# Splitting w2 in the second and third group, and w1 half an expert ahead

## The chip, the cores and the metric

The kernel runs on one core of a Trainium2 chip. The metric is the device time in microseconds of one execution, as the median of several runs. One execution was also recorded by the hardware profiler.

## The reference

Four batches of eight heads run a gated linear recurrence over 768 positions. Its result, reshaped to 3072 rows of 384, goes through four experts, each a two-layer network with a ReLU, weighted by normalised probabilities:

```python
for t in range(S):                                    # S = 768, D = 48
    state = alpha[:, :, t, :, None] * state + einsum('bhd,bhe->bhde', k[:, :, t], v[:, :, t])
    y[:, :, t] = einsum('bhd,bhde->bhe', q[:, :, t], state)
x = y.transpose(0, 2, 1, 3).reshape(3072, 384)
p = domain_probs / (domain_probs.sum(-1, keepdims=True) + 1e-09)
for e in range(4):                                    # w1: (4, 384, 1024), w2: (4, 1024, 384)
    h = maximum(x @ w1[e], 0)
    out += p[:, e:e + 1] * (h @ w2[e])
```

## The kernel before

**Units and groups.** The recurrence is cut into 24 units of 128 positions of one batch (`units`). Units are put into seven groups: two units in the first (`gi == 0`), four in each of the next five, two in the last (`gi == LAST == 6`). A task is one group through one expert; it is written (gi, e) here, so (1, 3) is the second group's fourth expert. The last two groups alternate expert by expert. A task is an *up* pass over eight column tiles of w1 (`up`, `fc` from 0 to 7) and a *down* pass over w2 (`down`).

**Precision by splitting.** From the second group on, each float32 product is made of three products of a faster type. A weight piece is split into three parts: `top` (rounded, made by ScalarE at L231), `rest` (VectorE, L233) and `both` (VectorE, L234). In the same way each hidden tile gets `top` by ScalarE's Relu (L739), `low` by VectorE (L761) and `dif` by VectorE (L766). The first group multiplies the whole weights in plain float32 (L731 up, L809 down), so it needs no parts.

**Pieces.** w1 and w2 are cut into 16 pieces each, four to an expert; a whole piece has 384 KB, its three parts 1152 KB. `load_piece(l, i)` puts a load on the SP queue: either of the whole (L214 for w1, L218 for w2), or of the three parts from `kept` in device memory (L195). `split_piece(l, i)` is a generator: its first step is ScalarE's L231, its second the two VectorE instructions and a store of the parts to `kept` on POOL's queue (L236). `background()` moves every open generator one step on and starts one more from the list `making`; it is called once behind each column tile of an up pass and at a few places of a down pass. So a split put on the list at tile `fc` has its ScalarE step behind that tile and its VectorE step behind the next.

**What is split when.** w1's 16 pieces are split during the first group, those of an expert while the expert is used: for the first and the fourth expert at tiles 1, 3, 5, 7, for the two others at tiles 2 and 5 and two in the down pass. Four w2 pieces, `EARLY` (the third and fourth of the second and third expert), are split in the first group too. The twelve others are split in the second group, each before the down pass that reads it; all 32 are stored, and from the third group on every piece is loaded as parts. The whole w2 pieces of the second, third and fourth expert of the second group lie in a buffer of the tag `hT`, of which there are four: the fourth hidden tile (column tiles 6 and 7) of the same expert takes that buffer next.

**Buffers.** Split w1 parts take turns in four buffers (tag `w1`), which the second group's loads of w1 parts use as well. At the end of the first group's last up pass the loads for (1, 0) go out in turn: w2 whole, w1 parts, w2 whole and so on. PSUM has four banks for products (`one`, `ops`; tag `g`) and two buffers for transposes, outputs and states (`tp`, `yps`, `sps`; tag `w`).

**Order.** The order of instructions on each engine is the order in which the program writes them. The attention of a unit is a generator of some 17 steps; `deal()` gives every step a due time on a clock of estimated matmul time, and `advance()` runs the steps that are due between matmuls. Loads of the raw q, k, v and alpha (`rq`, `rk`, `rv`, `ra`, L173) are written there and stand on SP's queue between those of the weights. A step's ScalarE copies are L503 (`qb`), L521 (`KT`), L598 and L602 (`lat`); VectorE's are L510, L512, L522 and L539; L667 to L670 update the state `st`.

Of the kernel before, what the change touches and what calls it, by code (L numbers as in the profile page):

```python
# [10 lines left out]
F32 = mybir.dt.float32  # L11
# [9 lines left out]
def kernel(  # L21
# [37 lines left out]
    nc = tc.nc  # L59

    B, H, S, D = q.shape
    E, DM, F = moe_w1.shape
# [9 lines left out]
    NQ = 4  # L72
# [69 lines left out]
    making = deque()  # L142
    splitting = []
# [17 lines left out]

    EARLY = {(1, 2), (1, 3), (2, 2), (2, 3)}


    def load(u, names):
# [3 lines left out]
        for nm in names:  # L171
# [4 lines left out]
    kept = [[dram.tile([P, 3, KC * QF], F32, name=f"kept{l}_{i}") for i in range(E * NQ)]  # L176
            for l in range(2)]
    wt = ({}, {})
    first_piece = lambda gi, e: (min(gi, LAST - 1) * E + e) * NQ

    AHEAD = 4


    SPLIT_AT = [(2, 5), (1, 3, 5, 7)]
    BESIDE = [{1: 2, 2: 3}, {2: 0, 4: 1}, {2: 0, 4: 1}, {2: 0, 3: 1, 4: 2, 5: 3}]

    def load_piece(l, i, beside=False):
        if i >= E * NQ * LAST:
            return
        gi, k = divmod(i, E * NQ)  # L190
        e, c = divmod(k, NQ)
        if gi > l or gi == 1 and (e, c) in EARLY:
            w = wt[l][i] = wts.tile([P, 3, KC * QF], F32R, name=f"w{l + 1}",
                                    bufs=AHEAD if l == 0 else NQ)
            nc.sync.dma_start(out=w.bitcast(F32), in_=kept[l][k])  # L195
            return
        if l == 1 and gi == 0 and not beside:
            return
        if l == 0:

            if e == 0:
                shared[c] = wts.tile([P, 3, KC * QF], F32R, name="w2", bufs=NQ)
            w = shared[c][:, 2 - e % 2].bitcast(F32)
        else:

            if gi == 1 and e > 0:
                if c == 0:
                    shared["w2"] = hid.tile([P, NQ, KC * QF], F32, name="hT", bufs=NQ)
                w = shared["w2"][:, c]
            else:  # L210
                w = hidden[c][:, gi].rearrange("p f n -> p (f n)")[:, :KC * QF].bitcast(F32)
        wt[l][i] = w
        if l == 0:
            nc.sync.dma_start(  # L214
                out=w.rearrange("p (c f) -> p c f", f=QF),
                in_=moe_w1[e].rearrange("(c p) f -> p c f", p=P)[:, :, c * QF:(c + 1) * QF])
        else:
            nc.sync.dma_start(  # L218
                out=w.rearrange("p (c d) -> p c d", d=DM),
                in_=moe_w2[e].rearrange("(c p) d -> p c d", p=P)[:, c * FPQ:(c + 1) * FPQ])  # L220

    def split_piece(l, i):
        k = i % (E * NQ)
        whole = wt[l].pop(i) if l == 0 else wt[l][i]
        if i >= E * NQ:
            w = wt[l][i] = wts.tile([P, 3, KC * QF], F32R, name="w2", bufs=NQ)
        else:
            w = wts.tile([P, 3, KC * QF], F32R, name="w1", bufs=AHEAD)
        top, both, rest = (w[:, part] for part in range(3))

        nc.scalar.activation(out=top, in_=whole, func=ACT.Copy, scale=LIFT)  # L231
        yield
        nc.vector.tensor_sub(rest, whole, top.bitcast(F32))  # L233
        nc.vector.scalar_tensor_tensor(out=both, in0=rest.bitcast(F32), scalar=4096.0, in1=whole,  # L234
                                       op0=ALU.mult, op1=ALU.add)
        nc.gpsimd.dma_start(out=kept[l][k], in_=w.bitcast(F32))  # L236

    def background():


        for piece in list(splitting):
            if next(piece, splitting) is splitting:
                splitting.remove(piece)
        if making and len(splitting) < 4:
            splitting.append(making.popleft())
            next(splitting[-1])
# [454 lines left out]
    def up(gi, e, fc, slots=None):  # L701
        n = len(groups[gi]) * P
        lo, hi = (slots.start * P, slots.stop * P) if slots else (0, n)
        begins, ends = lo == 0, hi == n
        c, f = divmod(fc, FPQ)
        i = first_piece(gi, e) + c
        if fc == 0 and begins:
            for k in range(NQ):
                hidden[k] = hid.tile([P, 3, FPQ, NT], F32R, name="hT", bufs=NQ)
        if gi == fc == 0 and begins:  # L710
            for k in range(NQ):
                load_piece(1, e * NQ + k, beside=True)
        if gi == 1 and fc in BESIDE[e]:
            making.append(split_piece(1, first_piece(gi, e) + BESIDE[e][fc]))
        if gi == 0 and ends and fc in SPLIT_AT[e in (0, E - 1)]:
            k = SPLIT_AT[e in (0, E - 1)].index(fc)
            making.append(split_piece(0, e * NQ + k))
        if gi == 0 and ends and e + 1 < E and fc == (0 if e == 0 else FCH // 2):
            for k in range(NQ):
                load_piece(0, (e + 1) * NQ + k)  # L720
        col = slice(f * P, (f + 1) * P)
        if gi > 0:
            w = wt[0][i].rearrange("p t (c f) -> p t c f", f=QF)[:, :, :, col]
        else:
            w = wt[0][i].rearrange("p (c f) -> p c f", f=QF)[:, :, col]
        parts = [hidden[c][:, part, f, lo:hi] for part in range(3)]
        whole = parts[2].bitcast(F32)
        one = ps.tile([P, NT], F32, name="one", tag="g", bufs=4)[:, :hi - lo]
        if gi == 0:
            for kc in range(KC):  # L730
                nc.tensor.matmul(one, lhsT=w[:, kc], rhs=xraws[gi][:, kc, lo:hi],  # L731
                                 start=(kc == 0), stop=(kc == KC - 1))
            nc.scalar.activation(out=whole, in_=one, func=ACT.Relu)
        else:
            for part in (1, 2, 0):
                for kc in range(KC):
                    nc.tensor.matmul(one, lhsT=w[:, part, kc], rhs=x_part(gi, part, kc),  # L737
                                     start=(part == 1 and kc == 0), stop=(part == 0 and kc == KC - 1))
            nc.scalar.activation(out=parts[0], in_=one, func=ACT.Relu, scale=TRIM)  # L739
            while finish:  # L740
                hidden_rest(*finish.popleft())
            finish.append((one, parts))
        while finish and fc == FCH - 1:
            hidden_rest(*finish.popleft())
        background()
        if f == FPQ - 1 and ends:
            if gi == 0:
                for k in range(AHEAD if i == E * NQ - 1 else 0):
                    load_piece(1, i + 1 + k)
                    load_piece(0, i + 1 + k)  # L750
            elif gi != LAST - 1:
                del wt[0][i]
                load_piece(0, i + AHEAD)
            while late:
                load_piece(1, late.popleft())
            while stores:
                stores.popleft()()
# [11 lines left out]
    def down(gi, e, slots, between):  # L769


        first = first_piece(gi, e)
        tiles = range(FCH)
        if gi == 0 and 0 < e < E - 1 and slots[0] == 0:
            making.extend(split_piece(0, first + k) for k in range(2, NQ))
            making.extend(split_piece(1, first + k) for k in range(NQ) if (e, k) in EARLY)
        if gi == 0 and e == E - 1 and slots[0] == 1:
            making.extend(split_piece(1, first + NQ + k) for k in range(NQ // 2))
        while gi == 1 and (making or splitting):
            background()  # L780

        if gi == 0:
# [6 lines left out]
        ends = {step[0]: n for n, step in enumerate(steps)}  # L789
        sums = {}  # L790
        for n, (slot, part, fc) in enumerate(steps):
            c, f = divmod(fc, FPQ)
# [10 lines left out]
            if part < 3:  # L803
                w = wt[1][first + c].rearrange("p t (c d) -> p t c d", d=DM)[:, part, f]
                h = h[:, part]
            else:
                w = wt[1][first + c].rearrange("p (c d) -> p c d", d=DM)[:, f]
# [5 lines left out]
            between.popleft()[1]()  # L813
        background()
        if slots[-1] == len(groups[gi]) - 1 and gi != LAST - 1:
            while gi == 0 and e < E - 1 and (making or splitting):
                background()

            for c in range(NQ):
                del wt[1][first + c]  # L820
                if gi == 0:
                    continue
                if c < NQ // 2 or gi in (1, LAST):
                    load_piece(1, first + NQ + c)
                else:
                    late.append(first + NQ + c)
# [88 lines left out]
    with tc.manual_schedule():  # L915
# [34 lines left out]
        for fc in range(FCH):  # L950
            up(0, 0, fc, slice(0, 1))
            if fc == FCH // 2:
                norm_probs()
            advance(cost(0, 0, 0) / 2)
        down(0, 0, [0], deque())
        while waiting:
            next(waiting.popleft()[2], None)
# [52 lines left out]
```

## Time and profile before

| | us |
|---|---|
| median of 3 runs | 1043.07 (1042.93 to 1044.69) |
| the profiled execution's own time | 1045.79 |
| its span, first to last instruction | 1044.0 |
| TensorE matmul busy | 1017.8 |
| VectorE busy | 639.3 |
| ScalarE busy | 441.5 |
| transfers: w<-kept | 148 of 1152 KB, median 8.4 to landing |
| transfers: kept<-w | 32 of 1152 KB, median 8.9 |
| transfers: hT<-in_moe_w_dram | 28 of 384 KB, median 6.2 |
| transfers: w<-in_moe_w_dram | 16 of 384 KB, median 6.4 |

Times within the profile count from the start of the span. In the timelines a row is start, duration, engine, line, operation, output<-inputs, shape and count; brackets give the idle time of the engine before it and what ended it. PE is TensorE, PEld its weight loads, DVE VectorE, ACT ScalarE; SPq is the sequencer of the SP queue. Neighbouring records of one kind are merged into one row. The first group runs to about 165 us, the second to about 341 us, and (2, 0) from there to about 383 us.

### The profile page before, as it was taken

How to read it: one execution, taken by the hardware profiler on the slowest of the kernel's cores; microseconds unless marked ns; L12 is line 12 of the kernel's file. 1: busy time of each engine (PE TensorE's matmuls, PEld its weight loads, DVE VectorE, ACT ScalarE, POOL GpSimd, SP SyncE). 2: the span in 40 equal slices, each digit the busy share in tenths (PEclk: the TensorE clock that was granted, in tenths of full speed). 3: DMA queues.
4: the chain of work that ended last, by engine and by line, in shares of the span. 5: the costliest groups of instructions: out<-in, count | busy, mean ns of one | idle time of the engine just before them, and what ended most of it. 6: DMA issues, size and time to landing. Idle time of an engine off the chain costs nothing.

```text
span 1044.0 us, 21240 instructions
## 1 busy us (share of the span) xinstructions
PE 1017.8 (97%) x8732; PEld 905.7 (87%) x8732; DVE 639.3 (61%) x1380; ACT 441.5 (42%) x971; POOL 35.6 (3%) x76
## 2 busy tenths in 40 slices
PE   7899997999999999999999999999999999999998
PEld 6777775889888899898898998998989989898998
DVE  4688886756869656556665555874756744334333
ACT  4687663453545344345343424454453422211111
POOL 2010011000000000000000000000000000000000
PEclk9999999899999999999999999999999999999999
DMA  9497999876958948668668569586594554544531
GB/s 196 127 360 257 292 360 404 314 270 205 370 181 285 361 154 303 255 210 317 233 208 332 187 244 349 188 295 238 167 364 173 218 213 155 208 182 181 202 161 46
DMA packets 144976, 254.79 MB, mean 244 GB/s; under 512 B 107088, under 2 KB 120784, under 8 KB 121840
## 3 DMA queue, kind: packets, MB, share of 16 engines
q1 hardware_dynamic: 138416, 211.03, 58.8%
q0 software_dynamic: 6016, 42.08, 10.0%
q8 instruction: 69, 1.13, 0.4%
q10 hardware_dynamic: 448, 0.33, 0.1%
q14 instruction: 27, 0.22, 0.1%
HBM read 210.94 MB, written 42.47 MB: 243 GB/s over the span
## 4 chain that ended last, share of the span: by engine, by line
PE 91%; DMA 2%; SPq 2%; DVE 2%; ACT 1%; issue 1%; ACTq 0%; DVEq 0%
PE ops L809 38%; PE one L737 34%; PE sc L529 6%; PE tp L267 4%; PE yps L624 3%; PE one L731 3%; DMA w<-kept 2%; SPq L218 2%; PE sps L659 1%; PE far L585 1%; ACT qb L503 1%; DMA rk<-in_k_dram 0%; DVE near L539 0%; PE sc L326 0%; SPq L195 0%
## 5 line engine op out<-in xcount | busy, mean ns | idle before, releaser
L809 PE MATMUL ops<-w,hT 128*128 128x384 f32 x2112 | 383.1, 339 | 0.8 <-ACT hT L739 0.8
L809 PEld LDWEIGHTS ops<-w,hT 128*128 128x128 f32 x2112 | 363.8, 188 | 3.0 <-ACT hT L739 1.3
L737 PE MATMUL one<-xT,w 128*128 128x512 f32 x1440 | 348.7, 396 | 5.0 <-DMA w<-kept 5.0
L737 PEld LDWEIGHTS one<-xT,w 128*128 128x128 f32 x1440 | 267.3, 189 | 62.7 <-DVE hT L761 4.5
L739 ACT ACTIVATE hT<-one 128x512 fp32r<-128x512 f32 (+1 forms) x192 | 107.8, 562 | 356.2 <-PE one L737 347.8
L761 DVE SCALAR_TENSOR_TENSOR hT<-one,hT 128x512 fp32r<-128x512 f32 (+1 forms) x192 | 122.6, 645 | 122.9 <-ACT hT L739 122.8
L503 ACT COPY qb<-QT 64x256 f32<-64x256 f32 x322 | 131.1, 407 | 53.1 <-DVE QT L482 26.4
L510 DVE TENSOR_TENSOR QT<-QT,dec 128x256 f32<-128x256 f32 x135 | 57.0, 422 | 101.1 <-ACT qb L503 100.6
L766 DVE SCALAR_TENSOR_TENSOR hT<-hT 128x512 fp32r<-128x512 f32 (+1 forms) x192 | 112.6, 638 | 0.1
L539 DVE COPY_PREDICATED near<-masks,sc 128x256 f32<-128x256 uint8 x138 | 73.9, 535 | 59.7 <-PE sc L529 56.4
L529 PEld LDWEIGHTS sc<-qb,KT 128*64 128x64 f32 x2208 | 69.7, 138 | 8.4 <-issue 6.8
L529 PE MATMUL sc<-qb,KT 128*64 128x64 f32 x2208 | 74.0, 223 | 2.0 <-ACT qb L503 1.2
L840 DVE SCALAR_TENSOR_TENSOR acc<-ops,p_all,acc 128x384 f32<-128x384 f32 x66 | 40.3, 615 | 55.1 <-PE ops L809 54.9
L521 ACT COPY KT<-KT 128x256 f32<-128x256 f32 x138 | 57.5, 416 | 3.4
L522 DVE TENSOR_TENSOR KT<-KT,dec 128x256 f32<-128x256 f32 x138 | 57.6, 417 | 0.5 <-PE sc L529 0.5
L731 PE MATMUL one<-xT,w 128*128 128x256 f32 (+1 forms) x240 | 47.7, 349 | 0.4 <-ACT xT L439 0.4
L809 PE MATMUL ops<-hT 128*128 128x384 f32 x128 | 47.5, 505 | 0.0
L731 PEld LDWEIGHTS one<-xT,w 128*128 128x128 f32 x240 | 39.2, 200 | 4.9 <-ACT xT L439 0.6
L849 POOL DMA_DIRECT2D out_dram<-acc x22 | 11.9, 541 | 694.1 <-DVE acc L840 690.8
L737 PE MATMUL one<-KT,w 128*128 128x256 f32 x288 | 34.6, 279 | 0.0
L737 PEld LDWEIGHTS one<-KT,w 128*128 128x128 f32 x288 | 34.4, 188 | 0.0
L624 PE MATMUL yps<-lat,rv 128*32 128x128 f32 x736 | 33.1, 273 | 1.3 <-ACT lat L602 1.3
(112 smaller groups left out, 721.7 us busy)
## 6 DMA issues: line engine op xcount, KB each, us to landing
w<-kept SPq DMA_DIRECT2D x148, 1152.0 KB, 8.4
kept<-w POOLq DMA_DIRECT2D x32, 1152.0 KB, 8.9
hT<-in_moe_w_dram SPq DMA_DIRECT2D x28, 384.0 KB, 6.2
w<-in_moe_w_dram SPq DMA_DIRECT2D x16, 384.0 KB, 6.4
rv<-in_v_dram SPq DMA_DIRECT2D x24, 192.0 KB, 8.2
ra<-in_alpha_dram SPq DMA_DIRECT2D x23, 192.0 KB, 6.3
rq<-in_q_dram SPq DMA_DIRECT2D x23, 192.0 KB, 5.8
rk<-in_k_dram SPq DMA_DIRECT2D x23, 192.0 KB, 6.3
```

The lines of the kernel that those rows point to most:

```text
L503: nc.scalar.copy(out=qb[rows, :, i, :].rearrange("p a (b r) -> p a b r", r=m), in_=qv[rows])
L521: nc.scalar.copy(out=new[:, :, :, 1, :], in_=old[:, :, :, 1, :])
L522: nc.vector.tensor_mul(new[:, :, :, 0, :], old[:, :, :, 0, :], spread(halved(decs[li])[:, :, :, 1], m))
L529: nc.tensor.matmul(out[HALF * s:HALF * (s + 1), 2 * p:2 * p + 2, :], lhsT=KTs[li][:, p, HALF * s:HALF * (s + 1)], rhs=qbs[li][:, p, :, QUA ...
L539: nc.vector.copy_predicated(near.rearrange("p a (b two r) -> p a b two r", two=2, r=m)[:, :, :, 1, :], mk.unsqueeze(1).broadcast_to([P, H, ...
L624: nc.tensor.matmul(yps[QUAD * j:QUAD * (j + 1), c, :], lhsT=lhsT, rhs=rhs, start=begins, stop=ends)
L731: nc.tensor.matmul(one, lhsT=w[:, kc], rhs=xraws[gi][:, kc, lo:hi], start=(kc == 0), stop=(kc == KC - 1))
L737: nc.tensor.matmul(one, lhsT=w[:, part, kc], rhs=x_part(gi, part, kc), start=(part == 1 and kc == 0), stop=(part == 0 and kc == KC - 1))
L739: nc.scalar.activation(out=parts[0], in_=one, func=ACT.Relu, scale=TRIM)
L761: nc.vector.scalar_tensor_tensor(out=low, in0=x, scalar=0.0, in1=top.bitcast(F32), op0=ALU.max, op1=ALU.subtract)
L766: nc.vector.scalar_tensor_tensor(out=dif, in0=low.bitcast(F32), scalar=-4096.0, in1=top.bitcast(F32), op0=ALU.mult, op1=ALU.add)
L809: nc.tensor.matmul(sums[slot], lhsT=h, rhs=w, start=(n == begins[slot]), stop=(n == ends[slot]))
```

## The change

The four `EARLY` pieces of w2 are no longer split in the first group: all 16 pieces of w2 are loaded whole and split in the second group. The four pieces of its first expert are not stored there; they are loaded whole once more in the third group, split in (2, 0), and stored then. `BESIDE` puts the four splits of an expert at tiles 2, 3, 4, 5 (for (1, 0), two are made in the down pass before and two at tiles 1 and 2). The w1 splits run half an expert ahead: two pieces of the next expert are split in the down pass of an expert, the two others at tiles 1 and 4 of its up pass. Of the w1 loads for (1, 0), two are issued behind tile 5 of the last up pass of the first group, and two behind tile 7, after the four w2 loads.

```diff
-    EARLY = {(1, 2), (1, 3), (2, 2), (2, 3)}
+    fresh = lambda gi, e: gi == 1 or (gi, e) == (2, 0)
...
-    SPLIT_AT = [(2, 5), (1, 3, 5, 7)]
-    BESIDE = [{1: 2, 2: 3}, {2: 0, 4: 1}, {2: 0, 4: 1}, {2: 0, 3: 1, 4: 2, 5: 3}]
+    SPLIT_AT = [{1: 2, 4: 3}, {1: 0, 3: 1, 5: 2, 7: 3}]
+    BESIDE = [{2: 0, 3: 1, 4: 2, 5: 3}, {1: 2, 2: 3}]
...
-        if gi > l or gi == 1 and (e, c) in EARLY:
+        if gi > l and not (l == 1 and fresh(gi, e)):
...
-            if gi == 1 and e > 0:
+            if gi > 1 or gi == 1 and e > 0:
...
-        nc.gpsimd.dma_start(out=kept[l][k], in_=w.bitcast(F32))
+        if (gi, k // NQ) != (1, 0):
+            nc.gpsimd.dma_start(out=kept[l][k], in_=w.bitcast(F32))
...
-        if gi == 1 and fc in BESIDE[e]:
-            making.append(split_piece(1, first_piece(gi, e) + BESIDE[e][fc]))
-        if gi == 0 and ends and fc in SPLIT_AT[e in (0, E - 1)]:
-            k = SPLIT_AT[e in (0, E - 1)].index(fc)
-            making.append(split_piece(0, e * NQ + k))
+        beside = BESIDE[(gi, e) == (1, 0)]
+        if fresh(gi, e) and fc in beside:
+            making.append(split_piece(1, first_piece(gi, e) + beside[fc]))
+        if gi == 0 and ends and fc in SPLIT_AT[e == 0]:
+            making.append(split_piece(0, e * NQ + SPLIT_AT[e == 0][fc]))
...
-                for k in range(AHEAD if i == E * NQ - 1 else 0):
+                for k in range(NQ if i == E * NQ - 1 else 0):
                     load_piece(1, i + 1 + k)
-                    load_piece(0, i + 1 + k)
+                for k in range(2 if e == E - 1 and c > 1 else 0):
+                    load_piece(0, E * NQ + 2 * (c - 2) + k)
...
-        if gi == 0 and 0 < e < E - 1 and slots[0] == 0:
-            making.extend(split_piece(0, first + k) for k in range(2, NQ))
-            making.extend(split_piece(1, first + k) for k in range(NQ) if (e, k) in EARLY)
+        if gi == 0 and e < E - 1 and slots[0] == (e == 0):
+            making.extend(split_piece(0, first + NQ + k) for k in range(2))
...
-        while gi == 1 and (making or splitting):
+        while fresh(gi, e) and (making or splitting):
             background()
...
-            while gi == 0 and e < E - 1 and (making or splitting):
-                background()
-
```

More of the change, by code (lines that the diff above doesn't have):

```diff
@@ L222, in split_piece @@
     def split_piece(l, i):
-        k = i % (E * NQ)
-        whole = wt[l].pop(i) if l == 0 else wt[l][i]
+        gi, k = divmod(i, E * NQ)
+        whole = wt[l][i]
         if i >= E * NQ:
```

## The prediction

> **What bounds the kernel now.** I read the page first: engines, then slices.
>
> ```profile
> PE 1017.8 (97%) x8732; PEld 905.7 (87%) x8732; DVE 639.3 (61%) x1380; ACT 441.5 (42%) x971; POOL 35.6 (3%) x76
> ...
> PEclk9999999899999999999999999999999999999999
> DMA  9497999876958948668668569586594554544531
> ```
>
> TensorE is busy 97% of the span, so only its 26 us of gaps, and stretches of lower clock, can be won. The clock row has one dip, in slice 8 (from 183 us), and the DMA engines are full in slices 5 to 7 just before it. So I asked for TensorE's waits, split at 200 us.
>
> ```profile
> PE one L737 <- DMA w<-kept: 5.0, 2, 3.9
> PE tp L267 <- DMA rq<-in_q_dram: 2.5, 2, 2.2
> ...
> PE ops L809 <- ACT hT L739: 0.8, 2, 0.5
> ```
>
> After 200 us only the last line is left: 0.8 us of waiting in 844 us. Whatever the change gains it gains before 200 us, and any new gap behind that is a loss. The windows of 5 us around the border between the first and the second group (columns: window, length, then PE, PEld, DVE, ACT, POOL busy, clock, DMA share, GB/s) and TensorE's timeline show where the time goes:
>
> ```profile
> 160.00:165.00 5.00, 3.34 (x8) 1.62 (x8) 2.98 (x7) 1.94 (x4) 0.00 (x0) 0.67 1.05 388
> ...
> 180.00:185.00 5.00, 1.08 (x4) 0.86 (x4) 3.40 (x7) 4.90 (x12) 0.00 (x0) 0.72 1.02 417
> 185.00:190.00 5.00, 5.00 (x17) 4.04 (x16) 3.89 (x8) 3.57 (x7) 0.54 (x1) 0.60 1.06 334
> ```
>
> ```profile
> 161.36 0.78 PE L267 MATMUL tp<-ident,rq 128*128 128x128 f32 x4 [2.20 <-DMA rq<-in_q_dram]
> 161.94 2.77 PE L809 MATMUL ops<-hT 128*128 128x384 f32 x4
> 165.83 6.37 PE L737 MATMUL one<-xT,w 128*128 128x512 f32 x27 [1.12 <-DMA w<-kept]
> ...
> 183.98 4.18 PE L737 MATMUL one<-xT,w 128*128 128x512 f32 x9 [3.92 <-DMA w<-kept]
> ```
>
> Three gaps, 2.20 + 1.12 + 3.92 = 7.24 us, all on transfers while the DMA share is 1.0. Behind the gaps the granted clock is 0.67, 0.72 and 0.60, and matmuls take longer: the four L809 records 2.77 us where four elsewhere take 1.46, the nine L737 4.18 where nine take 2.32, transposes 0.78 and 1.06 (187.96) where four take 0.60. That is 1.31 + 1.86 + 0.18 + 0.46 = 3.8 us. The border costs 11.0 us. The SP queue's timeline shows the jam:
>
> ```profile
> 141.35 16.52 SPq L218 DMA_DIRECT2D hT<-in_moe_w_dram  x1
> ```
>
> At 141 us one issue needs 16.5 us, so the four w1 pieces of the second group are issued only from 158 to 163, and the last lands 20.9 us later, when TensorE has been idle for 3.92. In 130 to 190 the DMA view lists 11 stores kept<-w (1152 KB each) and 22.79 MB in all, 380 GB/s.
>
> **The change part by part.** Prices of one split: ScalarE 0.84 (L231), VectorE 0.95 + 0.96 (L233, L234), one POOL issue and 1152 KB of store.
>
> *Four early w2 splits leave the first group; the first expert's four in the second are no longer stored.* In 130 to 190 the before has seven w1 and early w2 stores (131.9 to 152.2) and four of (1,0) (168.8 to 185.5). After, I count the last three w1 stores of the fourth expert, near 132, 138 and 145. Eight stores of 1.18 MB fewer are 9.4 MB, at 0.38 MB/us 25 us of all 16 engines, more than the jam. The transfers wanted stay: four w1 pieces and four w2 wholes, 6.3 MB or 16 us.
>
> *w1 pieces earlier.* Two are issued behind column tile 5 instead of 7, ahead of the w2 wholes. SP runs ahead of the matmuls there (at 141.35 it is already at tile 7's loads), so they go out near 141 instead of 158. They wait for buffers whose stores went out near 127 and 132 and land in 4.4 to 6.1 us by those rows, so no wait. The fourth piece waits for the store of 145, which by the rows nearby takes 9 us: 154. It lands near 163 and is wanted near 171. Behind it on SP stand the next unit's ra, rk and rq, wanted from 201 on: costs nothing. The w2 wholes now stand behind 2.3 MB more; ScalarE, which waited 6.3 + 1.9 + 6.6 us for them, wants the first near 157, and they land near 155 by the same count. With rq and w1 in time, the border's 11.0 us go; bounds 0 and 11.0. I keep 1.4 for what is late next (those ScalarE waits) and take **9.6 saved**, near the upper end, because 25 us of engine time are removed against a lateness of 3.9.
>
> The page "TensorE: Matmul & The Clock Gate" of the Trainium skill (its part 1 on the clock gate) has the clock halve after an idle window of about 3.4 us. Here a gap of 2.20 us is already followed by 0.67, so the row decides. By the rule only the last gap would be charged for the clock, and the sum would be 1.5 us smaller.
>
> *The first group without early splits.* Their VectorE time stands on the path once:
>
> ```profile
> 104.09 0.72 DVE L667 COPY st<-sps 64x192 f32<-64x192 f32 x2
> ...
> 104.91 0.63 PE L267 MATMUL tp<-ident,rk 128*128 128x128 f32 x4 [1.69 <-issue]
> ```
>
> TensorE says "issue", but rk's PSUM buffer (tag w, two buffers) is freed by L667, which ends at 104.81 and stands behind two early splits (L233 and L234 from 96.73 to 100.45), 3.8 us. Without them L667 can follow its matmul: 1.69 saved. At 152.03 a 0.71 wait for qb stands behind a ScalarE split that waited for a w1 buffer (0.76); that split is now three tiles earlier. Together **2.4 saved**; bounds 0 and 4.9 (the five gaps between 70 and 155: 1.18, 0.51, 1.69, 0.78, 0.71).
>
> *w1 splits half an expert ahead.* In most places they take a slot that another split had. The exception is the second expert's first two, which now come at 57 to 62 us, beside full engines (VectorE busy 4.93 of 5 us in 60 to 65). The first goes ahead of the last qb copy (57.36, ends 58.2, wanted at 58.4): 0.84 - 0.2 = 0.6 us of gap. The second pushes VectorE by 1.9 with about 1.5 of idle before the far product: 0.4. Their buffers are free (stores of 48.5 and 52.2 land in 5.9 and 7.2). **1.0 lost**; bounds 0 and 3.8 (two splits of 1.91 with no cover).
>
> *Two more splits each in (1,1) and (1,2), four in (2,0).* The wholes share a hidden buffer with the fourth hidden tile, so the Relu of column tile 6 waits until VectorE has split the fourth piece. Behind that Relu on ScalarE are the qb and KT copies and tile 7's Relu; TensorE waits when the down pass reaches tile 6. (1,3) does this already:
>
> ```profile
> 321.90 0.60 ACT L739 ACTIVATE hT<-one 128x512 fp32r<-128x512 f32 x1 [4.03 <-DVE w L234]
> ...
> 322.55 0.44 PE L809 MATMUL ops<-w,hT 128*128 128x384 f32 x1 [0.23 <-ACT hT L739]
> 323.53 1.48 PE L809 MATMUL ops<-w,hT 128*128 128x384 f32 x7 [0.54 <-ACT hT L739]
> ```
>
> A wait of 4.03 on ScalarE costs TensorE 0.77. Laying the added 1.91 us pieces into VectorE's timeline in order: in (1,1) tile 6's Relu moves from 232.3 to 236.7, the down pass wants it at 238.1: 0.3 at most. In (1,2) from 275.9 to 278.3, tile 7's to 280.3, wanted at 280.2: 0.3. In (2,0) two of the four fall into idle stretches (352.5 to 361 has 3.7 us), tile 7's Relu ends near 367.3, wanted at 366.6: 0.8. **1.4 lost**; bounds 0 and 3.8 + 3.8 + 7.6 = 15.2 if nothing hides a split.
>
> *Transfers later on.* Eight loads of 1152 KB become eight of 384 KB (median landing 8.4 and 6.2); stores stay 32, four of them now in (2,0). POOL has nothing else there. The third group's window 375 to 380 has no transfer at all, so nothing here; without that cover four stores cost 4 x 2.9 us of the engines.
>
> The page "DMA: Bandwidth & Descriptors" (section on measured bandwidth) asks for transfers of at least 1 MiB, which speaks against the smaller loads. Since one replaces one, even its fixed cost of 2 us each is no addition.
>
> **Sum.** 9.6 + 2.4 - 1.0 - 1.4 = 9.6 us. The profiled execution took 1045.79 (span 1044.0 and 1.8 around it) and would take 1036.2. It stands 2.7 us above the median of the runs, 1043.07; the gaps may be a little smaller in those, which the range covers. **Forecast 1043.07 - 9.6 = 1033.5.**
>
> **Rivals.** *The jam stays in part.* The DMA engines are also full from 52 to 80 and the 16 us of wanted transfers still meet three stores; if the w1 pieces land no sooner, only rq's part of the border goes (2.20 + 1.31), and the time is 1043.07 - (3.5 + 2.4 - 2.4) = 1039.6. For it: landing times of 20 us and more in that queue. Against it: the removed bytes. It also covers an order change that doesn't bring the loads forward.
>
> *All of it cancels.* VectorE's added work costs about 9 instead of 2.4: 1043 within 2 us. Nothing in the profile singles this out.
>
> *Slower.* One mechanism: Relu 6 behind the fourth split in (1,1), (1,2) and (2,0). Priced at its bound of 15.2 us it beats the other terms, 9.6 + 2.4 - 1.0 = 11.0, by 4.2: 1047. It decides once the three places together exceed 11 us, 3.7 each, five times what (1,3) shows. For it: VectorE is busy 9.7 of 10 us from 225 to 235 already. Against it: four PSUM buffers and the idle VectorE before each of these stretches.
>
> **How the numbers follow.** About 0.2%, 2.1 us, is what a measurement of this kernel tells from no change. Chances: forecast 0.68 (1029.5 to 1037.5; its lower end is 11.0 + 4.9 less 2.4), jam in part 0.14 (to 1041), cancelled 0.06, slower 0.12. Faster 0.82, same 0.06, slower 0.12. The range leaves out the last two: 1029.5 to 1041.0.
>
> **What would show it.** Right: no wait of L737 on w<-kept, no clock under 0.9 between 155 and 190, no SP issue of over 10 us near 141, three or four stores in 130 to 190, new waits of L739 on L234 of 3 to 5 us in (1,1), (1,2), (2,0) with TensorE losing under 1 us at each. Wrong: a w<-kept gap still at the border, or TensorE waiting for L739 over 3 us in all behind 200 us, or new gaps of over 3 us between 55 and 75.

## The result

The changed kernel took 1034.89 us (median of 4 runs, 1034.06 to 1035.43). The ratio to the kernel before is 0.9917, with a 95% interval of 0.9900 to 0.9934: faster by 8.2 us. The profiled execution took 1034.80 us, with a span of 1033.0; it stands at its kernel's median, while the profiled execution of before stood 2.7 us above its own.

The page after, engines and slices (a digit is a busy share in tenths):

```profile
PE 1015.6 (98%) x8732; PEld 903.9 (87%) x8732; DVE 645.9 (63%) x1388; ACT 443.9 (43%) x975; POOL 35.7 (3%) x76
...
PEclk9999999999999999999999999999999999999999
```

TensorE runs the same 8732 matmuls in 2.2 us less, and the dip of the clock row is gone. The windows around the border between the first and the second group say the same more finely (columns: window, length, busy time of PE, PEld, DVE, ACT, POOL, clock, DMA share, GB/s):

```profile
160.00:165.00 5.00, 5.00 (x24) 4.13 (x23) 4.93 (x9) 2.05 (x5) 0.54 (x1) 1.00 1.05 402
...
180.00:185.00 5.00, 5.00 (x83) 4.73 (x79) 4.63 (x11) 2.81 (x7) 0.00 (x0) 1.00 0.52 215
185.00:190.00 5.00, 5.00 (x34) 4.97 (x33) 4.43 (x12) 0.54 (x2) 0.00 (x0) 1.00 0.20 41
```

TensorE is busy for the whole of each window, at a clock of 1.00. The DMA engines are as full at 160 us as before, but drained at 185, where they were still full. TensorE's timeline over the border, where the three gaps were:

```profile
157.68 0.60 PE L268 MATMUL tp<-ident,rq 128*128 128x128 f32 x4
158.11 1.46 PE L810 MATMUL ops<-hT 128*128 128x384 f32 x4
159.11 6.60 PE L738 MATMUL one<-xT,w 128*128 128x512 f32 x27
...
167.16 8.46 PE L738 MATMUL one<-xT,w 128*128 128x512 f32 x36
```

No brackets: nothing waits for rq or for w<-kept, and four L810 take 1.46 where they took 2.77. (From L236 on, the lines named here are one higher than before; the experiments below shift lines by one or two more.) The SP queue's timeline shows why the loads are there:

```profile
141.09 2.29 SPq L195 DMA_DIRECT2D w<-kept  x2
143.43 2.81 SPq L218 DMA_DIRECT2D hT<-in_moe_w_dram  x4
146.63 10.23 SPq L195 DMA_DIRECT2D w<-kept  x2
```

Where one issue took 16.5 us before, the first six loads are now out by 146.2. The last row merges two issues and a wait: the third w1 load's issue takes 3.40 us; then SP waits 6.3 us for the store of 147.11, which lands at 156.37 and frees the buffer that the fourth w1 load takes; that load goes out at 156.52. Nobody is kept waiting by them. From 130 to 190 us there are 3 stores kept<-w, where there were 11, and 18.50 MB where there were 22.79.

What the change costs stands in the waits of TensorE, up to 200 us (first line) and behind it (last line; total, times, longest, in us):

```profile
PE tp L268 <- ACT AT L464: 2.5, 2, 1.8
...
PE ops L810 <- ACT hT L740: 2.0, 4, 0.7
```

### The profile page after: what moved, and what is told of

Same layout as the page of the kernel before. It is cut to its first block, busy times and chain, and to the rows that moved or that the text cites. A ratio compares the mean times of both kernels' runs of the same rounds, so it can differ in the third digit from the quotient of the medians.

```text
span 1033.0 us, 21246 instructions
## 1 busy us (share of the span) xinstructions
PE 1015.6 (98%) x8732; PEld 903.9 (87%) x8732; DVE 645.9 (63%) x1388; ACT 443.9 (43%) x975; POOL 35.7 (3%) x76
## 3 DMA queue, kind: packets, MB, share of 16 engines
q8 instruction: 69, 1.13, 0.4%
## 4 chain that ended last, share of the span: by engine, by line
PE 90%; DVE 5%; ACT 3%; issue 2%; POOL 0%; ACTq 0%; DVEq 0%; POOLq 0%
PE ops L810 39%; PE one L738 34%; PE sc L530 6%; PE tp L268 3%; PE yps L625 3%; PE one L732 2%; PE sps L660 1%; ACT qb L504 1%; PE far L586 1%; DVE w L233 1%; DVE w L234 1%; DVE near L540 1%; DVE QT L511 0%; PE idle L938 0%; DVE hT L763 0%
## 5 line engine op out<-in xcount | busy, mean ns | idle before, releaser
L810 PE MATMUL ops<-w,hT 128*128 128x384 f32 x2112 | 384.1, 339 | 2.0 <-ACT hT L740 2.0
L810 PEld LDWEIGHTS ops<-w,hT 128*128 128x128 f32 x2112 | 363.8, 188 | 5.2 <-ACT hT L740 3.4
L511 DVE TENSOR_TENSOR QT<-QT,dec 128x256 f32<-128x256 f32 x135 | 57.0, 422 | 98.2 <-ACT qb L504 97.7
L810 PE MATMUL ops<-hT 128*128 128x384 f32 x128 | 46.2, 494 | 0.0
```

What stands on the lines that cost most here:

```text
L810: nc.tensor.matmul(sums[slot], lhsT=h, rhs=w, start=(n == begins[slot]), stop=(n == ends[slot]))
```

## The experiments

The theory was the prediction's: the border waits because too many bytes stand in the DMA queues in front of the loads, and taking stores away cures it. Two rivals stood against it: that issuing two w1 loads two tiles earlier is what cures it, and that the splits' time on ScalarE and VectorE, not the transfers, held things up. Times in this section are medians; ratios are to the kernel before on the same chip, with the interval in brackets. The experiments ran on three chips, on which the kernel before took 1043.48 (w2_only, w1_only, order_back, store10), 1044.25 (w2_engines, w2_bytes, tile_sooner, lead_less_stored) and 1043.78 (the four others). So where medians of two chips are compared, the ratios or the same matmuls in the two traces are given beside them.

**One half of the change each.** The w2 half alone keeps the w1 splits and the order of the loads as before:

```diff
 # w2_only, against the changed kernel
-    SPLIT_AT = [{1: 2, 4: 3}, {1: 0, 3: 1, 5: 2, 7: 3}]
+    SPLIT_AT = [(2, 5), (1, 3, 5, 7)]
...
-                for k in range(2 if e == E - 1 and c > 1 else 0):
-                    load_piece(0, E * NQ + 2 * (c - 2) + k)
+                    load_piece(0, i + 1 + k)
...
-        if gi == 0 and e < E - 1 and slots[0] == (e == 0):
-            making.extend(split_piece(0, first + NQ + k) for k in range(2))
+        if gi == 0 and 0 < e < E - 1 and slots[0] == 0:
+            making.extend(split_piece(0, first + k) for k in range(2, NQ))
```

> The w2 part of the change alone: w1 is split and the loads of the second group are issued as before. Theory A (bytes): the 11 us at the border between the first and second group were lost because 11 stores of 1152 KB shared the DMA engines with the loads; here six of them are gone (two early w2 stores, four of (1, 0)), so TensorE waits for w<-kept under 1.5 us in all, the first-group gap near 105 us shrinks, the new gap near 66 us (1.84 in the changed kernel) is absent: 1034 to 1037 us. Theory B (order): the loads were late because they are issued late; then 6 to 11 us of the border stay: 1040 to 1044. Theory C (VectorE and ScalarE relieved of the early splits): as A, since they are gone here too.

Measured: 1033.10 (1032.16 to 1033.95), 0.9901 (0.9882 to 0.9920). The w2 half has the whole gain; its runs even lie below those of the changed kernel, though the two intervals overlap. Its border keeps one gap, 0.88 us for w<-kept at 161.08; the gap near 66 us that the changed kernel has is absent.

The w1 half alone keeps EARLY and all stores:

```diff
 # w1_only, against the kernel before
-    SPLIT_AT = [(2, 5), (1, 3, 5, 7)]
+    SPLIT_AT = [{1: 2, 4: 3}, {1: 0, 3: 1, 5: 2, 7: 3}]
...
-                    load_piece(0, i + 1 + k)
+                for k in range(2 if e == E - 1 and c > 1 else 0):
+                    load_piece(0, E * NQ + 2 * (c - 2) + k)
...
+        if gi == 0 and e < E - 1 and slots[0] == (e == 0):
+            making.extend(split_piece(0, first + NQ + k) for k in range(2))
...
-            making.extend(split_piece(0, first + k) for k in range(2, NQ))
```

> The w1 part alone, on the kernel before: w1 splits half an expert ahead and two of the w1 loads issued behind tile 5, but the four early w2 splits and all stores stay. Theory A (bytes): 9 of 11 stores between 130 and 190 us stay, so at least 5 of the border's 11 us stay, and the gap near 66 us of about 2 is added: 1038 to 1044. Theory B (order): the border is gone as in the changed kernel: 1034 to 1037. Theory C (engines): the early splits still stand on VectorE, the border stays: 1040 to 1044.

Measured: 1041.37 (1038.53 to 1042.88), 0.9980 (0.9968 to 0.9991): about 2 us. Its timeline, ScalarE's and TensorE's rows:

```profile
163.13 0.85 ACT L231 ACTIVATE w<-hT 128x768 fp32r<-128x768 f32 x1 [7.73 <-DMA hT<-in_moe_w_dram]
...
170.01 1.12 PE L585 MATMUL far<-qb,KT 128*64 128x128 f32 x8 [4.14 <-ACT qb L503]
```

TensorE no longer waits for w1, but the w2 wholes are now behind it in the jam: ScalarE waits 7.73 us for the first, the qb copy stands behind that split in ScalarE's order, and TensorE waits 4.14 for it. The jam is still there, with another load at its end: SP's issue of the first w1 load, at 145.90, takes 8.54 us.

The order of the loads alone, put back in the changed kernel:

```diff
 # order_back, against the changed kernel
-                for k in range(2 if e == E - 1 and c > 1 else 0):
-                    load_piece(0, E * NQ + 2 * (c - 2) + k)
+                    load_piece(0, i + 1 + k)
```

> The changed kernel with the loads for (1, 0) issued as before (all behind tile 7, w2 whole and w1 parts in turn). Theory A (bytes): nothing or up to 1.5 us slower than the changed kernel (1034.9), no wait for w<-kept over 1 us: 1034 to 1036.5. Theory B (order): 5 us or more of the border come back: 1039 to 1044. Theory C: as A.

Measured: 1034.75 (1034.39 to 1036.09), 0.9920 (0.9904 to 0.9936), and no wait for w<-kept. With the stores gone the order carries nothing. The first rival falls.

**The stores of (1, 0).** Four of the eight stores that the prediction counted are issued at the border or just behind it. Here they are made as before, and (2, 0) loads parts again:

```diff
 # store10, against the changed kernel
-    fresh = lambda gi, e: gi == 1 or (gi, e) == (2, 0)
+    fresh = lambda gi, e: gi == 1
...
-        if (gi, k // NQ) != (1, 0):
+        if True:
```

> The changed kernel, but the four w2 pieces of (1, 0) are stored there and loaded as parts in (2, 0), as before. Theory A (bytes): four stores from 160 to 175 us meet the last w1 loads of (1, 0), so 1 to 4 us of the border come back as waits for w<-kept; at (2, 0) the 1.2 us of waits behind the fourth split go: 1034 to 1038. Theories B and C: the stores do nothing, only the 1.2 us go: 1033 to 1034.5.

Measured: 1034.29 (1032.77 to 1034.70), 0.9908 (0.9891 to 0.9926), not to be told from the changed kernel, and no gap at the border. What the DMA view of this kernel says of 130 to 190 us is the surprise:

```profile
DMA packets 10864, 22.93 MB, mean 382 GB/s; under 512 B 6749, under 2 KB 8797, under 8 KB 8893
...
kept<-w POOLq DMA_DIRECT2D x7, 1152.0 KB, 9.1
```

It moves more bytes in that window than the kernel before (22.79 MB) and has no jam. So the sum of bytes over the stage isn't what decides: here a store issued at 163 us or later is in nobody's way.

**Work or bytes.** The next two put one side of the early pieces back into w2_only: the four splits, whose parts are neither stored nor read, and copies of 1152 KB within device memory, two each behind the second and the third expert's down pass, without any split.

```diff
 # w2_engines, against w2_only
+    EARLY = {(1, 2), (1, 3), (2, 2), (2, 3)}
...
-        if (gi, k // NQ) != (1, 0):
+        if (gi, k // NQ) != (1, 0) and (l, gi) != (1, 0):
...
+            making.extend(split_piece(1, first + k) for k in range(NQ) if (e, k) in EARLY)
 # w2_bytes, against w2_only
+            for k in range(2 if gi == 0 and 0 < e < E - 1 else 0):
+                nc.gpsimd.dma_start(out=again[2 * (e - 1) + k], in_=kept[0][k])
```

> The w2 part alone (w2_only, 1033.1), with the four early w2 splits done again in the first group, where they were before, but not stored and not used: 4 x 0.84 us on ScalarE and 4 x 1.91 on VectorE, no transfer. Theory A (bytes): the gap near 105 us (1.69 in the kernel before) comes back, the border does not: 1033.5 to 1036. Theory C (engines): the border comes back: 1039 to 1044.

> The w2 part alone (w2_only, 1033.1), with four unused copies of 1152 KB from device memory to device memory on POOL's queue, two at the end of the down pass of the second and two at that of the third expert of the first group, where the early stores were; no work on an engine. Theory A (bytes): waits of TensorE on loads, or of ScalarE on w2 wholes, come back at the border: 1037 to 1044. Theory C (engines): no change: 1032 to 1034.5.

Measured: w2_engines 1034.87 (1034.13 to 1035.71), 0.9904 (0.9879 to 0.9928); w2_bytes 1043.37 (1041.77 to 1045.29), 0.9987 (0.9971 to 1.0003). The splits cost 1.8 us between medians (0.3 by the ratios, which can't tell it from nothing). In the traces the same matmuls come 1.9 us later than in w2_only, all of it at one place: the gap of 1.71 us at 103.51, which the prediction had read in the trace of before, is back. The copies cost the whole gain. In w2_bytes, SP and TensorE:

```profile
144.57 13.48 SPq L219 DMA_DIRECT2D hT<-in_moe_w_dram  x1
...
147.39 2.90 PE L811 MATMUL ops<-hT 128*128 128x384 f32 x4 [3.97 <-DMA hT<-in_moe_w_dram]
```

The long issue is back, here of 13.48 us, though these transfers write nothing that anybody reads and engage none of the computing engines. A copy also reads what it writes, so it isn't the same transfer as a store; and the load that came late was another one, the w2 wholes of the first group's last expert. That made the next step necessary, with the true stores.

**Which stores.** The same four splits, all four stored; then only those of the second expert (issued near 99 and 101 us); then only those of the third (135.19 and 137.04 us):

```diff
 # against w2_engines; early_stored, early_stored_e1, early_stored_e2
-        if (gi, k // NQ) != (1, 0) and (l, gi) != (1, 0):
+        if (gi, k // NQ) != (1, 0):
+        if (gi, k // NQ) != (1, 0) and (l, gi, k // NQ) != (1, 0, 2):
+        if (gi, k // NQ) != (1, 0) and (l, gi, k // NQ) != (1, 0, 1):
```

> w2_engines (1034.9: the four early w2 splits made again, not used) with their four stores too, in the place and form they had in the kernel before. Theory A (bytes): the border's waits come back, 1039 to 1044, though the four (1, 0) stores are still left out. Rival (the copies of w2_bytes jam only because they come earlier, or read device memory as well): 1034.5 to 1037.

> As early_stored, but only the second expert's two early pieces are stored (near 99 us). If the border's jam is local, made by what is queued from 125 us on, these have drained by then: 1034.5 to 1036. If all traffic of the first group counts: 1037 to 1040.

> As early_stored, but only the third expert's two early pieces are stored (near 134 us). If the jam is local: nearly all of it comes back, 1038 to 1043. If all traffic of the first group counts: 1037 to 1040, as with the other two.

Measured: early_stored 1041.89 (1039.48 to 1044.44), 0.9977 (0.9963 to 0.9991); early_stored_e1 1035.33 (1033.63 to 1036.28), 0.9913 (0.9893 to 0.9933); early_stored_e2 1041.52 (1040.14 to 1044.22), 0.9980 (0.9966 to 0.9994). Against w2_engines at 1034.87, the second expert's two stores cost 0.5 us, within the spread, the third's two 6.6, all four 7.0 (by the ratios 0.9, 7.9 and 7.6). The two runs with two stores each, on one chip, are 6.2 apart. POOL's two early stores, SP and TensorE with the third expert's two:

```profile
135.19 0.53 POOL L238 DMA_DIRECT2D kept<-w  x1 [2.90 <-DVE w L235]
137.04 0.53 POOL L238 DMA_DIRECT2D kept<-w  x1 [1.33 <-ACT AT L647]
...
141.20 16.62 SPq L219 DMA_DIRECT2D hT<-in_moe_w_dram  x1
...
161.19 1.08 PE L269 MATMUL tp<-ident,rq 128*128 128x128 f32 x4 [2.21 <-DMA rq<-in_q_dram]
...
166.04 6.37 PE L740 MATMUL one<-xT,w 128*128 128x512 f32 x27 [1.32 <-DMA w<-kept]
```

and with the second expert's two:

```profile
140.06 1.68 SPq L219 DMA_DIRECT2D hT<-in_moe_w_dram  x1
...
164.23 2.33 PE L740 MATMUL one<-xT,w 128*128 128x512 f32 x9 [1.44 <-DMA w<-kept]
```

The first of these repeats the jam of the kernel before: an issue of 16.62 us against 16.52, a gap of 2.21 for rq against 2.20, of 1.32 for w<-kept against 1.12. The second has an issue of 1.68 us. Two stores, 2.4 MB, issued 4 to 6 us ahead of that issue make the difference; two like them 36 us earlier make none that can be measured.

The long issue is a sign of the jam and not all of it. The load of rq was issued before it began, at 137.13, 0.1 us behind the second store, and was slow all the same. The DMA view's line for it (the last column is the time from issue to landing), with the third expert's stores and with the second's:

```profile
rq<-in_q_dram SPq DMA_DIRECT2D x1, 192.0 KB, 23.9
...
rq<-in_q_dram SPq DMA_DIRECT2D x1, 192.0 KB, 6.6
```

Nor does the issue set when the last w1 load goes out. That load needs the buffer of the last w1 piece, whose store lands at 160.78 in the one kernel and at 160.84 in the other, and goes out at 162.28 and 160.97; what differs more is its way, 16.0 us against 12.3. A stored early piece also keeps its w1 buffer until its store has landed. That moves the last two w1 stores by about 1.2 us against w2_engines, but it can't hold rq, which uses no such buffer, and the copies of w2_bytes keep none.

One thing stays open. The third gap of before, 3.92 us at 183.98, is in neither kernel, and on the same chip the kernel before took 1043.78, 1.9 more than early_stored. Neither early_stored nor early_stored_e2 has the four stores of (1, 0). Those carry nothing where there is no jam (store10); whether they lengthen one that is there was not tried by itself.

**The costs.** tile_sooner starts the four w2 splits of an expert one tile sooner, so that the fourth is done before Relu 6 wants its buffer. lead_less_stored gives the second expert's w1 splits no lead, on top of store10's edit:

```diff
 # tile_sooner, against the changed kernel
-    BESIDE = [{2: 0, 3: 1, 4: 2, 5: 3}, {1: 2, 2: 3}]
+    BESIDE = [{1: 0, 2: 1, 3: 2, 4: 3}, {1: 2, 2: 3}]
 # lead_less_stored, against store10
-    SPLIT_AT = [{1: 2, 4: 3}, {1: 0, 3: 1, 5: 2, 7: 3}]
+    SPLIT_AT = [{1: 0, 3: 1, 5: 2, 7: 3}] * 2 + [{1: 2, 4: 3}] * 2
...
-        if gi == 0 and e < E - 1 and slots[0] == (e == 0):
+        if gi == 0 and 0 < e < E - 1 and slots[0] == 0:
```

> The changed kernel (1034.9) with the four splits of (1, 1), (1, 2), (1, 3) and (2, 0) one column tile sooner, at 1 to 4. My account of the later loss (Relu of tile 6 waits behind the fourth split): the 2.0 us of TensorE's waits for L740 behind 200 us go to under 0.7: 1033 to 1034.2. Rival (VectorE's added time itself is the loss, wherever it stands): waits of 1.5 us or more stay: 1034.5 to 1036.

> The changed kernel with the second expert's w1 splits not ahead (tiles 1, 3, 5, 7 of its own up pass) and the (1, 0) pieces stored there and loaded as parts in (2, 0). My account: the gap near 66 us (2.1 with its follow-up) goes, the one near 58 (0.35) too, and the 1.2 us at (2, 0): 1031 to 1033. Rival (the second expert's four splits in one up pass only move the gap to the latents near 75 us): 1033 to 1035.

Measured: tile_sooner 1032.17 (1031.76 to 1033.66), 0.9882 (0.9855 to 0.9910), and TensorE has no wait at all behind 200 us: the 2.0 us of waits on Relu 6 are gone, 0.8 of which the kernel before had too. From 200 us on, the same matmuls gain 3.1 us on the changed kernel (2.7 between medians, of different chips). lead_less_stored 1032.36 (1031.38 to 1033.83), 0.9882 (0.9854 to 0.9909): the gap near 66 us is gone, two others near 74 and 78 us are 1.18 and 1.25 where the changed kernel has 0.44 and 0.51, and the rest is a gain over store10: 1.9 between medians, of different chips, and 1.2 for the same matmuls from 40 us on.

**All three edits** of store10, lead_less_stored and tile_sooner:

```diff
 # all_three, against lead_less_stored
-    BESIDE = [{2: 0, 3: 1, 4: 2, 5: 3}, {1: 2, 2: 3}]
+    BESIDE = [{1: 0, 2: 1, 3: 2, 4: 3}, {1: 2, 2: 3}]
```

> The changed kernel with three edits together: the second expert's w1 splits not ahead, the (1, 0) pieces stored and loaded as parts in (2, 0), and the w2 splits one tile sooner. From the single runs: lead_less_stored 1032.4 less the 0.8 us of waits for L740 that are left behind 200 us: 1031.0 to 1032.5. Rival (the gains overlap): 1032 to 1033.5.

Measured: 1031.74 (1030.04 to 1031.96), 0.9875 (0.9853 to 0.9897). It is the fastest of all, and its interval ends below where that of the changed kernel begins. Its medians' distance from lead_less_stored, 0.6, and from tile_sooner, 0.4, is less than either edit brought by itself (2.7 and 1.9), and within the spread. In part the edits overlap: the 1.8 us that the splits of (2, 0) cost are taken away both by loading parts there, which store10's edit does, and by splitting a tile sooner. By the same matmuls all_three gains 1.4 over lead_less_stored behind 200 us and 1.6 over tile_sooner from 40 us on.

## Why the prediction was right

Forecast 1033.5, measured 1034.9; the sign, the place of the gain and the place of the costs were as forecast. To put a size to each step, the same matmuls are looked up in both traces and their times compared. The profiled execution of before was already 1.5 us later when the region around 40 us began, which isn't the change's. From there:

| step | forecast | measured |
|---|---|---|
| border, with its clock | 9.6 | 11.7 |
| the gap at 152 us | 0.71, in the 2.4 | 0.94 |
| the gap at 105 us | 1.69, in the 2.4 | 0.99 |
| the gap at 75 us | not named (bounds only) | 0.74 |
| the second expert's w1 lead | -1.0 | -2.63 |
| other small gaps before 146 us | 0 | -0.25 |
| behind 200 us | -1.4 | -2.2 |
| sum | 9.6 | 9.3 |

With the 1.5 of the start this is 10.8 of the 11.0 between the spans; the rest lies behind the last matmul. By medians the gain is 8.2. That the sums agree within 0.3 is partly luck: the border was sized 2.1 too low, and the two costs together 2.4 too low.

**The border: right in effect, wrong in what carries it.** The jam did go, and the 1.4 us kept back for what is late next were not needed: ScalarE waits 1.83 us for the first w2 whole at 157.06, and TensorE doesn't notice. But the step "eight stores fewer, 25 us of all 16 engines, against a lateness of 3.9" doesn't hold as it was argued. Of the eight stores between 130 and 190 us, the four of (1, 0) carry nothing by themselves (store10). Two are w1 stores that the lead moves forward, and w2_only, which leaves them where they were, is as fast. The other two, the third expert's early ones, carry 6.6 of the 7.0 that the four early ones bring (early_stored_e2). The second expert's two, issued at 99 and 101 us, were not among the eight and carry 0.5 (early_stored_e1). The prediction summed bytes over a stage of 60 us; what counts is what is queued in the few us before SP's loads. Its reading that the w1 pieces go out from 158 to 163 because of the long issue holds in part: their buffers are freed by stores that land at 151.95, 154.80, 157.87 and 160.85 in the kernel before, so the four could have gone at most 6, 6, 4 and 2 us sooner. Nor did the step "w1 pieces earlier" bring anything: order_back is as fast, and w1_only gains 2 us and moves the rest of the wait to another load. Without the jam both orders are early enough; with it neither is.

**The first group: the lead was mis-sized, 1.0 against 2.6.** The first piece's cost of 0.6 before the qb copy was right (0.56 measured). The other 2.07 are a chain that the prediction missed. The changed kernel's timeline, rows of three engines in order of start:

```profile
63.06 0.85 ACT L231 ACTIVATE w<-w 128x768 fp32r<-128x768 f32 x1 [1.13 <-DMA kept<-w]
63.59 0.96 DVE L234 SCALAR_TENSOR_TENSOR w<-w,w 128x768 fp32r<-128x768 f32 x1
64.47 0.42 DVE L511 TENSOR_TENSOR QT<-QT,dec 128x256 f32<-128x256 f32 x1
64.92 0.82 ACT L504 COPY qb<-QT 64x256 f32<-64x256 f32 x2 [1.01 <-DVE QT L511]
...
66.07 0.58 ACT L464 COPY AT<-tp 128x512 f32<-128x512 f32 x1
...
66.71 0.66 PE L268 MATMUL tp<-ident,rq 128*128 128x128 f32 x4 [1.84 <-ACT AT L464]
```

Two splits of 1.9 us lie back to back on VectorE (60.72 to 64.5). L511 stands behind them, ScalarE's qb copy waits 1.01 us for L511, and the AT copy behind that is late; it frees the PSUM buffer that TensorE's next transpose needs. The prediction laid VectorE's 1.9 against its idle 1.5, and so took 0.4, and didn't follow who waits for the instructions behind. The next split on ScalarE also waited 1.13 us for an earlier store to read the w1 buffer: the prediction had called these buffers free.

The 105 gap gave 0.99 of its 1.69. The reading was right, since w2_engines brings the gap back (1.71) and w2_only hasn't got it; in the changed kernel 0.68 of it remain, but on another holder, ScalarE's AT copy, behind a qb copy that a w1 split at 99.97 had held up.

**Behind 200 us: right.** Relu 6 waits for the fourth split in all three places, 5.92, 2.65 and, in (2, 0), 6.93 us; the sign was named as 3 to 5, so the places are right and the lengths spread wider. TensorE was to lose under 1 us at each; by the same matmuls it loses 0.2 in (1, 1), 0.2 in (1, 2) and 1.8 in (2, 0), where 0.3, 0.3 and 0.8 were forecast. In (2, 0), timeline:

```profile
353.99 0.60 ACT L740 ACTIVATE hT<-one 128x512 fp32r<-128x512 f32 x1 [6.93 <-DVE w L234]
...
354.64 0.44 PE L810 MATMUL ops<-w,hT 128*128 128x384 f32 x1 [0.68 <-ACT hT L740]
355.61 1.32 PE L810 MATMUL ops<-w,hT 128*128 128x384 f32 x6 [0.54 <-ACT hT L740]
```

ScalarE's 6.93 us cost TensorE 0.68 + 0.54 of waits, about 1.2 of the 1.8. So the rival that ends slower had its waits but not its price: it needed 11 us, and the three places brought 2.2. Only the 1.2 in (2, 0) stand in the rows as added waits (2.0 in all after, 0.8 before); the other 1.0 show in no row of a wait, only in the later matmuls. tile_sooner confirms the cause by taking the waits away, and the lost time with them.

**The rivals.** "The jam stays in part" is ruled out for this kernel by the rows at the border, but is the truth of w1_only, the case of a change of order that doesn't take the right stores away. "All of it cancels" isn't the case either.

## What to carry to other kernels

When a load comes late, look up what was put into the queues in the few microseconds before its issue, rather than add up the bytes of the stage: here two stores of eight mattered, those 4 to 6 us ahead. When work is moved onto an engine with idle time beside it, the idle time in sum proves nothing; follow the instruction queued right behind the new work to whoever waits for it. And take a bundled change apart: its w2 half alone was no slower than the whole, and three small edits to its costly parts made it faster.

## What the runs showed of the hardware

One SP issue of a 384 KB load lasted 16.5 us in the kernel before, 16.6 and 17.1 in the kernels that store the third expert's two or all four early pieces, and 13.5 with the copies. All other issues of such loads, in all kernels, took 0.4 to 2.9 us. Two stores of 1152 KB are 2.4 MB, some 6 us of the engines at 380 to 420 GB/s, yet between early_stored_e1 and early_stored_e2 the issue grows by 15 us, from 1.68 to 16.62. What exactly holds the sequencer isn't shown by any row. A long issue alone is no loss: one of w<-kept takes 7.89 us near 766 us before and 7.83 near 756 after, and TensorE doesn't wait there.

The five kernels with the jam, the kernel before among them, scatter more from run to run: the standard deviation of their times is 1.1 to 2.4 us (runs of 12 to 23), that of the others 0.6 to 1.0 (4 to 6 runs). The four runs of the kernel before beside the result alone gave 0.8, so the difference shows only over many runs.

The gap of 2.20 us for rq in the kernel before, followed by a clock of 0.67, was no accident: in early_stored_e2 the same gap, 2.21, is followed by the same clock in its window:

```profile
160.00:165.00 5.00, 3.53 (x8) 1.91 (x8) 2.69 (x5) 1.84 (x4) 0.00 (x0) 0.66 1.05 415
```

Gaps of 1.84 (66.71 in the changed kernel) and 1.85 (161.80 in early_stored, again for rq) are followed by matmuls of the usual length, in early_stored four L812 in 1.46. Where between 1.85 and 2.20 us it turns, and whether the length of the gap alone decides, isn't shown. The Trainium skill's page "TensorE: Matmul & The Clock Gate" (its part 1) puts the idle window behind which the clock halves at about 3.4 us. These rows show the drop after less, and the rows decide.
